# Attention over channels and a GELU layer on one core: an order of issue written out step by step, more seven-product sets, and sums of squares by accumulating DMAs

## The chip, the core and the metric

The kernel runs on one NeuronCore of a Trainium2 chip. PE (TensorE) multiplies matrices, ACT (ScalarE) applies functions, DVE (VectorE) does elementwise arithmetic and transposes of 32 by 32 tiles, POOL (GpSimd) and SP (SyncE) mostly issue DMAs. Each engine works through its own queue in order; semaphores tie the queues together. Matmul results land in PSUM, eight banks of 128 x 512 fp32; everything else on the core lies in SBUF.

The metric is the device time of one launch in microseconds, the median of several runs. The profile is of one further execution, whose own time is given beside its span.

## The reference

```python
# q, k, v: (4, 6080, 256) fp32; tau = 1; w_in: (256, 2048); w_out: (2048, 256)
qn = q / (norm(q, axis=1) + 1e-6)          # norms over the 6080 tokens
kn = k / (norm(k, axis=1) + 1e-6)
s = kn.transpose(0, 2, 1) @ qn / tau       # (4, 256, 256)
a = exp(s - s.max(-1)); a /= a.sum(-1) + 1e-9
x = (v @ a).reshape(24320, 256)
h = x @ w_in
g = 0.5 * h * (1 + tanh(c * (h + 0.044715 * h**3)))
out = g @ w_out                            # (24320, 256) fp32
```

## The kernel before

**Tiling.** Per batch the attention matrix is only 256 x 256, so the kernel folds it into the first weights: AW = a @ w_in (256 x 2048, bf16), made once a batch. Then h = v @ AW, the GELU, and the product with w_out run over blocks of 512 tokens, 12 to a batch, the last one with 448; 48 blocks in all, numbered n, with block n % 12 of batch n // 12. The 2048 columns of a block are eight *pairs* of two 128-column groups. For one pair `mm1` does four matmuls of 512 columns into a double bank and `gelu` turns it into bf16 in `g`.

**Sets.** Two pairs can be made together in seven half-size products (a Strassen-like scheme over two halves of the tokens, two of the inner dimension and two pairs). `SETS` names the pairs that go together: 1 with 2, and 5 with 6. `small` does product m (1 to 7) as two matmuls of 256 columns, into a double bank `qp` or into the single bank `rb` (tag "s"). The steps between are in `set_step`: cq and y5 are copies on ACT, ap and ax are additions on DVE, Gq, Gr and Gx the GELUs of the parts. `sums_w` prepares differences of AW once a batch, `sums_v` differences of v once a block. Blocks 0 and 1 of all have no sets, block 2 has one, blocks 10 and 11 of the first three batches have none, every other block has two (`sets_of`).

**Second product.** The product with w_out is always done in seven products, M1 to M7, each in two halves A and B of four matmuls with 256 columns, into banks "r" and "p". T1 to T4 are the differences of g that it needs (`sums_1`, `sums_2`, on DVE); cq, y5, ap, ax, c11a are copies and additions of its results, c11 to c22 the transposes into the output tile, after the fourth of which `store` issues four DMAs on SP. Most of this runs one block after the h that it uses, some of it two.

**The next batch.** While a batch is multiplied, q and k of the next one arrive in chunks of six rows for each partition (`load_one`, on POOL's queue, which converts fp32 to bf16). In blocks 1 to 8 the Gram matrix of q and k is summed in PSUM bank "a" (`gram_row`, row0 to row5), ACT squares the chunk (qsq, ksq), and `fold` adds the squares up on DVE: an addition in bf16 of half the rows to the other half, then three fp32 additions into the running sum ACC of 128 x 512. After the last chunk `ss_cols` sums ACC over the partitions on PE, and a chain of small steps follows in blocks 9 to 11 (`norms`, `k_factors`, `k_row`, `scores_b`, `scores_c`, `row_sums`, `aw_part`), which ends with the next AW.

**Order.** The scheduler is off: instructions stand on each engine in the order in which the program issues them. Before, three lists of steps served all blocks: `GRAM`, `PLAIN` and `NO_SETS` (L604 to L620). A step like "M1A-1" means M1A of the block before; "w0m1" product 1 of set 0; "g3" and "G3" matmuls and GELU of pair 3; "vs+1" the differences of v of the next block. `todo` keeps a set of what is done, and `extras` hangs loads and the chain on the steps e0 to e7. "w" steps of a set that a block does not have turn into `mm1` and `gelu` of its pairs.

Of the kernel before, what the change touches and what calls it, by code (L numbers as in the profile page):

```python
# [3 lines left out]

# [13 lines left out]
def kernel(  # L18
# [31 lines left out]
    addp = ctx.enter_context(tc.tile_pool(name="addp", bufs=1))  # L50
# [3 lines left out]
    vts = ctx.enter_context(tc.tile_pool(name="vts", bufs=4))  # L54
# [6 lines left out]
    xp = ctx.enter_context(tc.tile_pool(name="xp", bufs=1))  # L61
    cp = ctx.enter_context(tc.tile_pool(name="cp", bufs=1))
# [121 lines left out]
    def fold_rows(b, c):  # L184

        n = len(rows_of(b, c))
        if n == 8:
            a1 = addp.tile([128, 4, 512], BF16, tag="a1")
            nc.vector.tensor_add(a1, SQ[b, c][:, 0:4, :], SQ[b, c][:, 4:8, :])
            SQ[b, c] = a1  # L190
            n = 4
        SQR[b, c] = n
# [3 lines left out]
    def fold(b, c, k):  # L196


        n = len(rows_of(b, c))
        half = n // 2  # L200
        if k == 1:
            sq = SQ.pop((b, c))
            a1 = addp.tile([128, 4, 512], BF16, tag="a1", name=f"a1_{b}_{c}")
            nc.vector.tensor_add(a1[:, 0:half, :], sq[:, 0:half, :], sq[:, half : 2 * half, :])
            terms = [a1[:, i, :] for i in range(half)]
            if n % 2:
                terms.append(sq[:, n - 1, :])
            if b in ACC:
                terms.append(ACC[b])
            FOLD[b, c] = terms  # L210
            return
        terms = FOLD[b, c]
        if len(terms) < 2:
            return
        last = len(terms) == 2
        if last and b not in ACC:
            ACC[b] = accp.tile([128, 512], FP32, tag="acc", name=f"acc{b}")
        o = ACC[b] if last else addp.tile([128, 512], FP32, tag=f"a{2 + k % 2}", name=f"f{k}_{b}_{c}")
        nc.vector.tensor_add(o, terms[0], terms[1])
        FOLD[b, c] = [o] + terms[2:]  # L220
# [37 lines left out]
    def ss_cols(b):  # L258

        SS[b] = pM.tile([128, 4], FP32, tag="a", name=f"ss{b}")  # L260
        for j in range(4):
            nc.tensor.matmul(SS[b][:, j : j + 1], lhsT=ACC[b][:, j * 128 : j * 128 + 128],
                             rhs=ones_f[:, 0:1], start=True, stop=True)
# [38 lines left out]

    def pe_vt(n, tag):

        ps = pM.tile([128, 2, BLK], BF16, tag=tag, name=f"vt_ps{n}")
# [4 lines left out]
        vT = vts.tile([128, 2, BLK], BF16, tag="vT", name=f"vT_pe{n}")  # L310
        nc.vector.tensor_copy(vT[:, 0, :], ps[:, 0, :])
        nc.vector.tensor_copy(vT[:, 1, :], ps[:, 1, :])
        vt_tiles[n] = vT
# [35 lines left out]
    def norms(b):  # L349

        sv = smx.tile([128, 4], FP32, tag="sv")
        nc.vector.tensor_copy(sv, SS[b])
        rt = smx.tile([128, 4], FP32, tag="rt")
        nc.gpsimd.tensor_tensor(rt, sv, halves, op=ALU.pow)
# [20 lines left out]
    def k_row_pe(b):  # L375
        dg, rh = NRM[b]
        ps = pM.tile([128, 256], FP32, tag="a", name=f"rk{b}")
        nc.tensor.matmul(ps, lhsT=ones_f, rhs=dg, start=True, stop=True)
        S = G[b]
        for jc in range(2):  # L380
            nc.vector.tensor_mul(S[:, jc, :], S[:, jc, :], ps)
        NRM[b] = (S, rh)

    def scores_b(b):
        S, rh = NRM.pop(b)
        th = smx.tile([128, 2, 256], FP32, tag="th")
        for jc in range(2):
            nc.scalar.activation(th[:, jc, :], S[:, jc, :], AF.Tanh, scale=rh[:, jc : jc + 1])
        TH[b] = th

    def scores_c(b, step):
# [7 lines left out]
        step -= 1  # L399
        dn = DN[b]  # L400
        piece = dn[:, step // 2, step % 2 * 128 : step % 2 * 128 + 128]
        nc.vector.reciprocal(piece, piece)
        if step == 3:
            eT = smx.tile([128, 2, 256], BF16, tag="eT")
            nc.vector.scalar_tensor_tensor(eT, th, 1.0, dn, op0=ALU.add, op1=ALU.mult)
            ET[b] = eT

    DN = {}

    def row_sums(b):  # L410
        ps = pM.tile([128, 2], FP32, tag="a", name=f"sums{b}")
        for ic in range(2):
            for jc in range(2):
                nc.tensor.matmul(ps[:, ic : ic + 1],
                                 lhsT=ET[b][:, jc, ic * 128 : ic * 128 + 128],
                                 rhs=ones_bf[:, 0:1], start=jc == 0, stop=jc == 1)
        rs = smx.tile([128, 2], FP32, tag="rs")
        nc.vector.reciprocal(rs, ps)
        RS[b] = rs

    AW = {}

    def aw_part(b, fs, ic, eng, tag="a"):
        if b not in AW:
            AW[b] = awp.tile([128, 2, D], BF16, tag="aw", name=f"aw{b}")
        ps = pM.tile([128, 512], FP32, tag=tag)
        for jc in range(2):
            nc.tensor.matmul(ps, lhsT=ET[b][:, jc, ic * 128 : ic * 128 + 128],  # L428
                             rhs=win_bf[:, jc, fs * 512 : fs * 512 + 512],
                             start=jc == 0, stop=jc == 1)  # L430
        o = AW[b][:, ic, fs * 512 : fs * 512 + 512]
        if eng == "act":
# [15 lines left out]
    GS, HP = {}, {}  # L448

# [8 lines left out]
    SIDE = {}  # L458

    def pair_of_banks(n, p, name):  # L460

        if (n, p) not in SIDE:
            side = SIDE.get("next", 0)
            k = sets_of(n)
            if k == len(SETS):
                turns = [x for x in range(PAIRS) if x not in [b for _, b in SETS]]
            else:
                turns = [int(x[1]) if x[0] == "g" else SETS[int(x[1])][x[2:] == "m7"]
                         for x, _ in order_of(n)
                         if x[0] == "g" or x[0] == "w" and (x[2:] == "m5" if int(x[1]) < k else x[2:] in ("m1", "m7"))]  # L470
            for x in turns:
                SIDE[n, x] = side
# [593 lines left out]
```

## Time and profile before

| what | value |
|---|---|
| device time, median of 3 runs | 718.33 us (718.33 to 719.25) |
| profiled execution: its own time, its span | 717.09 us, 715.3 us |
| granted TensorE clock | 0.998 |
| matmuls of `mm1` (L495), of sets (L564), of the second product (L716) | 904, 1106 and 3 narrow ones, 2688 |
| DMA traffic of POOL's queue, of SP's | 39.46 MB, 37.67 MB |
| first matmul, last matmul | at 10.2 us, at 708.3 us |

A row of the groups reads: line, engine, operation, output <- inputs, shape, count | busy us, mean ns of one | idle us of the engine just before, and what ended it. A row of the timeline: start, duration, engine, line, operation, tiles, shape, count of instructions merged into it, and in brackets the idle time before it. A row of DMA issues: output <- input, issuing queue, count, KB each, and the median us from issue to landing.

### The profile page before, as it was taken

What the parts mean: (1) busy time and instruction counts of PE and PEld (TensorE: products, weight loads), DVE (VectorE), ACT (ScalarE), POOL (GpSimd) and SP (SyncE); (2) the same over time, 40 slices, a digit from 0 to 9 for tenths busy, and PEclk for the clock granted to TensorE, in tenths of its full rate; (3) what the DMA queues carried; (4) which work ended last, traced back from release to release, by engine and by line L of the source; (5) the groups of instructions that cost most, each with busy time, mean ns of one, the idle gap of its engine ahead of it and who ended that gap; (6) DMA issues with size and microseconds to landing.
All of it is one profiled execution on the core that took longest, in us unless ns stands there. A gap on an engine that the chain in (4) does not pass through costs nothing.

```text
span 715.3 us, 13755 instructions
## 1 busy us (share of the span) xinstructions
PE 682.2 (95%) x5335; PEld 515.5 (72%) x5335; DVE 610.5 (85%) x1174; ACT 595.3 (83%) x828; POOL 69.8 (10%) x131
## 2 busy tenths in 40 slices
PE   3898999999999999999999999999999999999995
PEld 2755777777667777777767787777766777777784
DVE  4489799998987999999878899999897788888885
ACT  5387799998768999999868999999876888888883
POOL 4320011100001111010000111110000000000000
PEclk9999999999999999999999999999999999999999
DMA  9999578973567888974557699887355245363414
GB/s 242 207 249 145 97 113 124 131 115 58 98 93 127 106 126 138 135 132 66 93 90 111 104 133 132 125 127 120 58 92 96 49 82 93 64 113 59 72 31 85
DMA packets 162273, 79.28 MB, mean 111 GB/s; under 512 B 150464, under 2 KB 153280, under 8 KB 161216
## 3 DMA queue, kind: packets, MB, share of 16 engines
q0 software_dynamic: 13440, 39.46, 34.5%
q1 hardware_dynamic: 147664, 37.67, 32.5%
q10 hardware_dynamic: 1104, 1.28, 0.5%
q8 instruction: 41, 0.67, 0.4%
q14 instruction: 24, 0.20, 0.1%
HBM read 78.91 MB, written 36.83 MB: 162 GB/s over the span
## 4 chain that ended last, share of the span: by engine, by line
PE 79%; DVE 11%; DMA 6%; issue 2%; ACT 1%; POOL 0%; DVEq 0%; POOLq 0%; ACTq 0%
PE h L495 22%; PE r L716 20%; PE p L716 15%; PE rb L564 9%; PE qp L564 7%; PE G L230 4%; DMA t<-in_k_dram 3%; DMA wst<-in_moe_w_out_dram 2%; PE ps L428 2%; DVE ot L740 1%; DMA t<-in_q_dram 1%; DVE t L677 1%; DVE t L693 1%; DVE t L689 1%; DVE t L691 1%
## 5 line engine op out<-in xcount | busy, mean ns | idle before, releaser
L716 PEld LDWEIGHTS <-wcomb 128*128 128x128 bf16 x2688 | 262.1, 98 | 63.0 <-issue 8.1
L505 ACT ACTIVATE g<-h 128x1024 bf16<-128x1024 f32 (+1 forms) x226 | 227.6, 1011 | 43.6 <-PE h L495 41.0
L495 PE MATMUL h<-vT,aw 128*128 128x512 bf16 (+1 forms) x840 | 212.1, 375 | 0.7 <-ACT g L584 0.7
L716 PE MATMUL r<-t,wcomb 128*128 128x256 bf16 (+1 forms) x1152 | 164.7, 271 | 3.1 <-DVE c L731 2.5
L495 PEld LDWEIGHTS <-aw 128*128 128x128 bf16 x904 | 88.4, 98 | 65.6 <-issue 1.6
L716 PE MATMUL p<-g,wcomb 128*128 128x256 bf16 (+1 forms) x704 | 94.2, 271 | 0.0
L584 ACT ACTIVATE g<-qp 128x1024 bf16<-128x1024 f32 (+1 forms) x79 | 80.2, 1015 | 9.5 <-PE qp L564 9.2
L176 ACT ACTIVATE sq<-t 128x1536 bf16<-128x1536 bf16 (+4 forms) x59 | 79.5, 1361 | 9.6 <-DMA t<-in_q_dram 9.6
L564 PEld LDWEIGHTS <-sw 128*128 128x128 bf16 x632 | 61.5, 98 | 29.0 <-issue 5.3
L579 DVE TENSOR_TENSOR qp<-rb,yw 128x512 f32<-128x512 f32 (+1 forms) x79 | 54.9, 695 | 24.9 <-ACT x L725 16.1
L691 DVE TENSOR_TENSOR t<-g 128x1024 bf16<-128x1024 bf16 (+1 forms) x96 | 64.5, 672 | 0.0
L693 DVE TENSOR_TENSOR t<-t,g 128x1024 bf16<-128x1024 bf16 (+1 forms) x96 | 64.3, 670 | 0.0
L564 PE MATMUL rb<-tv,sw 128*128 128x256 bf16 (+1 forms) x316 | 60.1, 272 | 3.6 <-DVE qp L579 3.4
L230 PE MATMUL G<-t 128*128 128x256 bf16 (+1 forms) x368 | 60.5, 272 | 2.0 <-DMA t<-in_k_dram 1.9
L582 DVE TENSOR_TENSOR xw<-rb,yw 128x512 f32<-128x512 f32 (+1 forms) x79 | 54.3, 687 | 8.7 <-PE rb L564 8.1
L689 DVE TENSOR_TENSOR t<-g,t 128x1024 bf16<-128x1024 bf16 (+1 forms) x96 | 60.9, 666 | 0.0
L589 ACT ACTIVATE g<-rb 128x512 bf16<-128x512 f32 (+1 forms) x79 | 47.1, 597 | 16.4 <-PE rb L564 13.9
L136 POOL DMA_DIRECT2D vb<-in_v_dram x46 | 23.1, 502 | 356.6 <-PE h L495 356.6
L677 DVE TENSOR_TENSOR t<-g 128x2048 bf16<-128x2048 bf16 (+1 forms) x48 | 57.1, 1190 | 0.2 <-ACT g L592 0.2
L716 PE MATMUL r<-g,wcomb 128*128 128x256 bf16 (+1 forms) x384 | 55.9, 271 | 0.3 <-DVE ot L740 0.3
L716 PE MATMUL p<-t,wcomb 128*128 128x256 bf16 (+1 forms) x384 | 52.1, 271 | 1.5 <-DVE c L731 1.5
L574 ACT ACTIVATE qp<-rb 128x512 f32<-128x512 f32 (+1 forms) x79 | 46.4, 588 | 5.5 <-PE rb L564 2.4
(127 smaller groups left out, 852.2 us busy)
## 6 DMA issues: line engine op xcount, KB each, us to landing
out_dram<-ot SPq DMA_DIRECT2D x176, 128.0 KB, 3.2
vb<-in_v_dram POOLq DMA_DIRECT2D x42, 256.0 KB, 5.2
t<-in_q_dram POOLq DMA_DIRECT2D x22, 384.0 KB, 7.0
t<-in_k_dram POOLq DMA_DIRECT2D x22, 384.0 KB, 4.6
wst<-in_moe_w_out_dram POOLq DMA_DIRECT2D x2, 1024.0 KB, 10.9
t<-in_q_dram POOLq DMA_DIRECT2D x3, 512.0 KB, 14.9
t<-in_k_dram POOLq DMA_DIRECT2D x3, 512.0 KB, 16.7
out_dram<-ot SPq DMA_DIRECT2D x12, 112.0 KB, 2.5
```

Source lines behind the costliest of these rows:

```text
L176: nc.scalar.activation(o, t[:np_, r, :], AF.Square)
L230: nc.tensor.matmul(G[b][:, jc, :], lhsT=qt[:np_, r, jc * 128 : jc * 128 + 128], rhs=kt[:np_, r, :], start=first and jc == 0, stop=jc == 1, ...
L495: mm = nc.tensor.matmul(hp[:, u, :cols], lhsT=AW[b][:, cc, fc * 128 : fc * 128 + 128], rhs=vt_tiles[n][:, cc, :cols], start=cc == 0, stop= ...
L505: nc.scalar.activation(gs(n)[:, 2 * p : 2 * p + 2, :cols], HP.pop((n, p))[:, :, :cols], AF.Gelu_apprx_tanh)
L564: nc.tensor.matmul(acc[:, u * hc : u * hc + hc], lhsT=lhs[:, u * 128 : u * 128 + 128], rhs=rhs, start=m in (1, 5) and u == 0, stop=u == 1, ...
L579: nc.vector.tensor_add(qp(n, i)[:, 1, :c], RB[n, i][:, :c], YW[n, i][:, :c])
L584: nc.scalar.activation(gs(n)[:, 2 * pa : 2 * pa + 2, :c].rearrange("p u (t x) -> p t u x", t=2), QP.pop((n, i))[:, :, :c].rearrange("p t ( ...
L677: nc.vector.tensor_sub(t1[:, :, :hc], quarter(n, 0, 1), quarter(n, 0, 0))
L689: nc.vector.tensor_sub(o, quarter(n, 1, 1, f0, f1), ts[1][:, f0:f1, :hc])
L691: nc.vector.tensor_sub(o, quarter(n, 1, 1, f0, f1), quarter(n, 0, 1, f0, f1))
L693: nc.vector.tensor_sub(o, ts[2][:, f0:f1, :hc], quarter(n, 1, 0, f0, f1))
L716: nc.tensor.matmul(ACCS[n, acc][:, :hc], lhsT=wcomb[:, w, fc, :], rhs=x, start=first and k == 0, stop=k == 3, skip_group_check=True)
```

## The change

All lists and the machinery around them go. A string of steps stands for each block: 31 strings, and `WINDOW` says which of them block n uses (those of blocks 8 to 19 serve the second and third batch too). A step is now one instruction or a tight group on one engine, and the loop does nothing but run them in order. Three of the strings stand below.

Blocks 10 and 11 get two sets as the others have; blocks of the last batch get three, with pairs 4 and 7 in the third, whose weight differences lie in the buffers of the squares. The banks of sets' `rb` are "s" and "s", and "s", "a", "s" in the last batch. The tiles of ap and ax (`yw`, `xw`) lie in buffers of q and k in the last batch, and `yw` gets two buffers elsewhere.

`fold` keeps its bf16 addition, of three rows to three. Its result goes by a DMA from POOL's queue into ACC, now 128 x 3 x 512 fp32: a plain converting copy for the first chunk, an accumulating one for the seven others. `fold_last` (fl1, fl2) adds the three parts on DVE before `ss_cols`. The transposed tiles of v have three buffers instead of four. The last block's end keeps another order of its products.

```diff
-    vts = ctx.enter_context(tc.tile_pool(name="vts", bufs=4))
+    vts = ctx.enter_context(tc.tile_pool(name="vts", bufs=3))
...
-    def fold(b, c, k):
...
-        o = ACC[b] if last else addp.tile([128, 512], FP32, tag=f"a{2 + k % 2}", name=f"f{k}_{b}_{c}")
-        nc.vector.tensor_add(o, terms[0], terms[1])
-        FOLD[b, c] = [o] + terms[2:]
+    def fold(b, c):
+        assert len(rows_of(b, c)) == 6
+        sq = SQ.pop((b, c))
+        a1 = a1p.tile([128, 3, 512], BF16, tag="a1", name=f"a1_{b}_{c}")
+        nc.vector.tensor_add(a1, sq[:, 0:3, :], sq[:, 3:6, :])
+        FOLD[b, c] = a1
+
+    def fold_dma(b, c):
+        first = b not in ACC
+        if first:
+            ACC[b] = accp.tile([128, 3, 512], FP32, tag="acc", name=f"acc{b}")
+        nc.gpsimd.dma_start(out=ACC[b], in_=FOLD.pop((b, c)),
+                            **({} if first else {"accum_op": ALU.add}))
+
+    def fold_last(b, i):
+        nc.vector.tensor_add(ACC[b][:, 0], ACC[b][:, 0], ACC[b][:, i])
...
+    SIDE = ({0: 0, 2: 0, 4: 0, 6: 0}, {0: 0, 3: 0, 5: 0, 7: 0}, {0: 0, 3: 0, 5: 0}, {0: 0, 5: 0, 3: 0})
+    R_BANK = ("", "s", "ss", "sas")
...
     def sets_of(n):
-        blk = n % NB
-        if n == 2:
-            return 1
-        if n < 2:
-            return 0
-        return 0 if n // NB < B - 1 and blk in (10, 11) else 2
+        return (0, 0, 1)[n] if n < 3 else 3 if n // NB == B - 1 else 2
...
-    SETS = ((1, 2), (5, 6))
+    SETS = ((1, 2), (5, 6), (4, 7))
...
+    def set_buffer(n, i, xy):
+        if n // NB == B - 1:
+            return qkp.tile([128, 512], FP32, tag="qk"[xy == "x"], name=f"{xy}w{n}_{i}")
+        return {"x": xp, "y": ywp}[xy].tile([128, 512], FP32, tag=f"{xy}w", name=f"{xy}w{n}_{i}")
...
+        def loads(n, p):
             b, blk = divmod(n, NB)
             gate = GATE[0]
             if p == 0 and PE_BLOCKS <= n + 2 < NN:
                 load_vt(n + 2)
             if p == 0 and n + 3 < NN:
                 cast_v(n + 3, gate)
+            if p in (2, 5) and b + 1 < B and blk < len(chunks_of(b + 1)):
+                load_one(b + 1, blk, p // 5, gate)
...
         for n in range(NN):
+            for x in ORDER[WINDOW[n]].split():
+                m = re.match(r"([A-Za-z]+\d*[A-Za-z]*\d?)(?:([+-])(\d+))?$", x)
+                step(m[1], n + {None: 0, "+": 1, "-": -1}[m[2]] * int(m[3] or 0))
+
+WINDOW = [
+    0, 1, 2, 3, 4, 5, 6, 7, 8, 9, 10, 11, 12, 13, 14, 15, 16, 17, 18, 19, 8, 9, 10, 11,
+    12, 13, 14, 15, 16, 17, 18, 19, 8, 9, 20, 21, 22, 23, 24, 25, 26, 27, 27, 27, 27, 28,
+    29, 30,
+]
+ORDER = [
...
+    """g0 w0cq c11a-2 w0y5 e0 row2-1 w0m6 G0 row4 w0ap row4-1 row1-1 M1B-1 T2b-1 ksq e2 w0m7
+    M1A-1 T3a-1 g3 w0ax cq-1 M5B-1 T3b-1 G3 w0m4 M5A-1 c11-2 T4b-1 w0m3 w0Gr w0m2 row1 e5
+    T4a-1 w0Gq w1m5 M6A-1 c22-2 w1m1 vs+1 M6B-1 y5-1 w1cq g4 ap-1 w1y5 w1m6 qsq row5-1 w1ap
+    M3A-1 M3B-1 w1m3 c12-1 w1m7 w0Gx row5 f1 w1m2 G4 M7A-1 M2B-1 w1ax fd M2A-1 w1Gq T1a M7B-1
+    w1m4 w1Gx g7 ax-1 w1Gr c22-1""",
+    """g0 G7-1 c11a-2 T3a-1 e0 w0m1 row3-1 G0 T2a-1 M4B-2 row0-1 T2b-1 w0m5 M4A-2 w0cq e2 row2-1
+    c21-2 M5A-1 w0y5 fl1 w0m6 g3 w0ap M5B-1 fl2 G3 w0m7 M1A-1 w0ax w0m2 gc M1B-1 vs+1 y5-1 e5
+    w0m4 w0m3 w0Gr ss T4b-1 cq-1 c11-2 w0Gq w1m5 sv w1m1 T3b-1 M6B-1 pow M6A-1 T4a-1 w1cq g4
+    w1y5 ap-1 kf w0Gx w1m6 M3A-1 G4 w1ap M7B-1 T1a M7A-1 kr w1m7 g7 ax-1 w1ax krp G7 w1m2 S0+1
+    M3B-1 S1+1 w1m3 w1Gx w1m4 c12-1 w0m5+1 w1Gr vs+2 M4A-1 M4B-1 w1Gq T3b M2B-1 c21-1 w0m1+1
+    M2A-1 T3a w0cq+1""",
...
+    """g0 T1a-1 w2Gr-1 e0 w1m1 G0 M4A-2 c11a-2 w0m5 w0m1 T3a-1 M4B-2 w0cq e2 M5B-1 c21-2 w0y5
+    w1m5 T2a-1 w0m6 w2Gx-1 M5A-1 w0ap M1A-1 w1y5 M1B-1 T2b-1 w1cq w0m7 cq-1 w0m2 w0ax w0m3
+    y5-1 w1m6 e5 w0Gq M6A-1 w1ap w0m4 M6B-1 T3b-1 w0Gr w1m7 w2m5 ap-1 w1m2 w2y5 w1m3 w1ax w2m1
+    M3A-1 w2cq vs+1 M3B-1 w1Gq M7B-1 c12-1 w2m6 c11-2 M7A-1 w1Gx w2ap w1m4 w0Gx g3 c22-2 w1Gr
+    T4b-1 w2m7 G3 w2m3 w2ax M2A-1 w2m2 ax-1 M2B-1 w2Gq T4a-1 w2m4""",
...
+]
```

The strings shown are those of block 8 and block 9 of a batch, where the last chunk is added and the chain of the next batch begins, and the one of four blocks of the last batch.

## The prediction

> **What bounds the kernel now.** I read the busy table first, then busy time by stage, then the rows of the operations that the change counts up or down, then the DMA issues.
>
> ```profile
> PE 682.2 (95%) x5335; PEld 515.5 (72%) x5335; DVE 610.5 (85%) x1174; ACT 595.3 (83%) x828; POOL 69.8 (10%) x131
> ```
>
> PE is busy 95% of the span, but these are averages. The view of busy time by stretch (us; PE, PEld, DVE, ACT, POOL with counts, then clock, DMA share, GB/s) shows where the other 5% is:
>
> ```profile
> 40.00:80.00 40.00, 35.73 (x238) 22.69 (x236) 33.27 (x60) 30.39 (x36) 4.70 (x9) 1.00 0.91 171
> 80.00:160.00 80.00, 80.00 (x646) 62.86 (x645) 75.12 (x144) 75.78 (x104) 9.54 (x18) 1.00 0.81 121
> 160.00:200.00 40.00, 37.90 (x276) 26.73 (x274) 35.25 (x67) 30.65 (x47) 2.57 (x4) 1.00 0.48 83
> ...
> 560.00:700.00 140.00, 140.00 (x1120) 109.10 (x1118) 119.19 (x230) 119.73 (x179) 3.89 (x8) 1.00 0.40 68
> ```
>
> In the long stretches (the blocks with Gram rows at 80 to 160, the last batch at 560 to 700) PE is never free. It is free in the start and around the joint of two batches (160 to 200). In the Gram stretch VectorE and ScalarE stand at 94 and 95%; in the last batch both have 15% left. Is "never free" also "at its peak"? Matmul records overlap, so I take starts in the timeline of PE:
>
> ```profile
> 632.74 1.04 PE L716 MATMUL p<-g,wcomb 128*128 128x256 bf16 x8
> 633.61 0.38 PE L564 MATMUL rb<-vT,aw 128*128 128x256 bf16 x2
> 633.83 0.60 PE L716 MATMUL r<-t,wcomb 128*128 128x256 bf16 x4
> 634.27 1.03 PE L495 MATMUL h<-vT,aw 128*128 128x512 bf16 x4
> 635.13 0.38 PE L564 MATMUL rb<-tv,sw 128*128 128x256 bf16 x2
> ```
>
> Eight matmuls of 256 columns take 633.61 - 632.74 = 0.87 us, 0.109 each; four of 512 take 0.86, 0.216 each. Time goes by columns, with almost nothing per instruction. **A rule of the Trainium skill speaks against using this:** "Perfetto Trace Analysis", section "Identifying the Most-Contended Engine", says that matmul busy share misleads and that the weight-load share tells the headroom. That is 62.86/80 = 79% in the Gram stretch and 78% in the last batch: by the rule a fifth of PE is free, other engines bind, and columns taken away give 0. By the start times PE has nothing left there, and columns count in full. I go by the start times.
>
> Start to start, PE's idle time comes to 11.4 us around the three joints (4.3 in 160 to 260, 3.8 in 320 to 400, 3.3 in 500 to 560), 5.2 in 40 to 80, and 1.4 after 700.
>
> **The change, part by part.**
>
> *More sets.* A set makes two pairs of 128-column groups with 14 matmuls of 256 columns in place of 8 of 512: 14 x 0.1087 = 1.52 against 8 x 0.216 = 1.73 us of PE, 0.206 less. By the two instruction lists there are 24 more: two in each of blocks 10 and 11 of three batches (12), a third in each block of the last batch (12); 7 of them have 448 columns. PE: 17 x 0.206 + 7 x 0.18 = **-4.8 us**, all of it where PE is busy or waits little. What the others pay:
>
> ```profile
> L505 ACT ACTIVATE g<-h 128x1024 bf16<-128x1024 f32 x198 | 202.3, 1024 | 32.2 <-PE h L495 30.2 <-DVE aw L435 1.8
> L584 ACT ACTIVATE g<-qp 128x1024 bf16<-128x1024 f32 x77 | 78.3, 1017 | 8.7 <-PE qp L564 8.4
> L579 DVE TENSOR_TENSOR qp<-rb,yw 128x512 f32<-128x512 f32 x77 | 53.7, 697 | 24.1 <-ACT x L725 16.1 <-ACT yw L577 8.0
> L582 DVE TENSOR_TENSOR xw<-rb,yw 128x512 f32<-128x512 f32 x77 | 53.0, 689 | 8.2 <-PE rb L564 7.7
> ```
>
> ScalarE: two GELUs (2.05) become copy 0.59, copy 0.60, GELUs 1.02, 0.60 and 0.62 (rows L574, L577, L584, L589, L592): +1.37 a set. VectorE: +0.70 + 0.69 = 1.39. A block of the last batch lasts 12.65 us (the casts of v start at 627.95 and 640.59). ScalarE and VectorE are busy there 119.73/140 and 119.19/140 of it, 10.8 each. A third set makes that 12.2 at most, PE's columns 12.65 - 0.21 = 12.4. It fits, by 0.2 us. The third set has its own bank for its neighbour ("a", free when no Gram runs), so its chain of PE, ScalarE, VectorE and PE again does not queue behind the first two. If the cover fails by 0.25 us a block, 12 x 0.25 = 3 us eat the gain.
>
> *Sums of squares.* The row L219 goes, 69 fp32 additions (24 + 21 + 21 + 3), about 47.1 us of VectorE:
>
> ```profile
> L219 DVE TENSOR_TENSOR f<-a x24: 684/686/693, 67.5 to 505.4; 128x512 f32<-128x512 bf16 x24
> L219 DVE TENSOR_TENSOR f<-f,a x21: 650/678/681, 88.1 to 506.7; 128x512 f32<-128x512 f32 x21
> L219 DVE TENSOR_TENSOR acc<-f,acc x21: 684/685/693, 94.3 to 507.4; 128x512 f32<-128x512 f32 x21
> ```
>
> Six return at the ends (4.1). With 33.3 for the sets, 5.9 for six more blocks' differences of v and 1.2 for one more weight set, VectorE does 47.1 - 44.5 = 2.6 us less in all, but 2 us less in each Gram block and more at the joints and in the last batch. ScalarE does +33.0 - 2.7 (copies of the old order without sets) + 1.5 (one square moved to it) = 31.8 more, 88% of the span. Worth to PE of VectorE's relief in the Gram blocks: 0, PE never waited there.
>
> Added are 24 DMAs on POOL's queue, some 0.54 us of issue each as its other DMAs (13 us more, POOL is at 10%). POOL holds each until VectorE's addition and the former accumulation are done; behind it stand loads of q, k and casts of v. Neighbours are 8 us or more apart but for chunks 4 and 5 (7 us), and what waits has a block of slack: 0. **The dangerous wait** is VectorE's first closing addition of each batch, which needs the last accumulation landed. Behind it stands the addition that the next set's matmul needs. Counting PE's columns in the list from the last issue to that addition gives 5.2 us. How long does an accumulation take? No row shows one. It writes 128 x 1536 fp32, 786 KB, and reads as much again. Near rows (last column: us from issue to landing):
>
> ```profile
> vb<-in_v_dram POOLq DMA_DIRECT2D x42, 256.0 KB, 5.2
> t<-in_q_dram POOLq DMA_DIRECT2D x22, 384.0 KB, 7.0
> t<-in_k_dram POOLq DMA_DIRECT2D x22, 384.0 KB, 4.6
> wst<-in_moe_w_out_dram POOLq DMA_DIRECT2D x2, 1024.0 KB, 10.9
> t<-in_q_dram POOLq DMA_DIRECT2D x3, 512.0 KB, 14.9
> ```
>
> The skill's "DMA: Bandwidth & Descriptors", section "Anatomy of one DMA", fits 2.0 us + bytes/436 GB/s: 3.8 us, an estimate from that page, no wait. By the rows of q and k, which read 786 KB too, it is 4.6 to 7.0; the largest row allows 14.9, in the crowded start. I take 7.0: no q or k is loaded in that block, but the destination is read as well. With 0.5 for the issue VectorE waits 2.3. PE has up to 1.5 us of other work in the list (m6, g3, M5B) before the matmul that needs VectorE's next addition; I take 1.3 as its lead, so PE loses 1.0: **+3 us** for three batches (bounds 0 and, at 14.9, +27).
>
> *One list for all blocks.* Steps now stand singly: the softmax chain of the next batch is cut into single instructions over blocks 9 to 11, factors and copies apart from their matmuls. The waits that it can remove are those 11.4 us, such as 0.49 at 168.0 behind four folds of L219, 0.62 at 170.7, 0.75 at 196.7 where PE has just made row sums and stands before the reciprocal. From rows' spacings every block of the new list needs more PE than VectorE or ScalarE time, but four by 0.5 at most and block 11 of the first batch (VectorE 13.7, PE 11.8, it prepares two weight sets): +1. I take 60% of the joints' idle as gone, **-7**; bounds 0 and -11.4. In the start weights' preparation and the first sets are cut apart too: half of 5.2, **-2.5**. Against it I set 0.05 us a block for unevenness, +1.8: the old orders left 0.00. At the end the last product is now followed by an addition and a transpose, before by a transpose alone: +0.4. Pools: v's transposed tiles go from 4 buffers to 3; the load for block n+2 then waits for block n-1's last matmul, and has 18 us to land in 5.5: 0.
>
> Sum: -4.8 + 3 - 7 + 1 - 2.5 + 1.8 + 0.4 = -8.1. The profiled execution took 717.09 (span 715.3 and 1.8 around it), so 709.0; the median of the runs shown, 718.33, is 1.2 above it: **710**.
>
> **Rivals.**
> 1. *Only the columns pay.* New waits at the joints replace the old: 718.3 - 4.8 + small losses = 714. For it: VectorE is the fuller engine at the joints (35.25 of 40), and sets add work just there. Against: four folds leave that very place.
> 2. *The accumulation is late* (the slower side). Each batch loses the landing less 6.0 us (5.2 + 1.3 - 0.5). The rest of the change brings 11.1, so it decides from a loss of 3.7 a batch, a landing near 9.7 us. At 12 to 15: 3 x 6 to 3 x 9 = 18 to 27, some 725 to 734. For it: 10.9 and 14.9 in the rows. Against: DMA share is 0.48 there, 1.06 in the start.
> 3. *ScalarE binds.* With 88% on average and 95% in Gram blocks the one-by-one order leaves 0.2 to 0.3 us of PE idle in 36 blocks, 7 to 11 us: 717 to 722.
> 4. *The change does less than it says:* by the lists it has 103 sets against 79 and 24 accumulations, so this is out.
>
> **How the numbers follow.** Forecast 0.54; rival 1 0.15; rival 2 0.16; rival 3 0.15 (half of it slower, a third the same). A difference under 0.2% (1.4 us) can't be told from none. Faster: 0.54 + 0.15 + 0.02 = 0.71; same 0.06; slower 0.23. The forecast's own range is 703 (all joints gone) to 715. To hold 8 in 10 it goes from 702 to 722, which leaves out most of rival 2.
>
> **What would show it.** Right: PE's records of the h matmuls fall from 904 to 712, PE idle near 160 to 200 halves, blocks of the last batch start 12.4 us apart. The dangerous wait is the idle time before the addition into acc, released by a DMA: under 3 us each. I am wrong if that is above 5, if ScalarE is at 97% or more in Gram blocks with PE idle beside it, or if blocks of the last batch stay at 12.65.

## The result, and the profile after

| what | before | after |
|---|---|---|
| device time, median (lowest to highest), four runs each | 718.33 us (717.46 to 719.25) | 713.95 us (712.45 to 715.93) |
| profiled execution: its own time, its span | 717.09, 715.3 us | 714.2, 712.3 us |
| granted TensorE clock | 0.998 | 0.990 |

The ratio is 0.994, with an interval from 0.9913 to 0.9968: the changed kernel is 4.4 us faster, about half of what was forecast. A run over 1.5% above the fastest of its kernel counts as slow and is left out of ratios, though not of medians: one of e1 (714.05 us), one of e12 (807.62) and one of before (1207.34, beside e5 to e8). The first lines of the page after, busy time and the clock in 40 slices of 17.8 us:

```profile
PE 680.7 (96%) x5479; PEld 532.1 (75%) x5479; DVE 608.6 (85%) x1180; ACT 618.5 (87%) x894; POOL 92.0 (13%) x155
...
PEclk9998999999999999999999999999999999999999
```

VectorE has 1.9 us less, as worked out (2.6). ScalarE's rows add up to 31.1 more, as worked out (31.8); its busy time, in which overlapping records count once, rose by 23.2. POOL has 22 more, not 13. PE's busy time hardly fell, though its work shrank by the columns of 24 sets. The row of the clock, which the prediction never used, says why one should look further: it has an 8 in its fourth slice, and the mean clock went down. Busy time by stretch of the kernel after (us; PE, PEld, DVE, ACT, POOL with counts, then clock, DMA share, GB/s):

```profile
40.00:60.00 20.00, 13.31 (x62) 6.30 (x61) 12.87 (x21) 8.92 (x9) 1.62 (x3) 0.84 0.80 194
...
100.00:120.00 20.00, 16.51 (x121) 12.26 (x120) 11.51 (x22) 14.35 (x19) 3.01 (x5) 0.91 0.85 176
80.00:160.00 80.00, 76.51 (x600) 59.14 (x598) 64.24 (x121) 72.11 (x94) 14.12 (x23) 0.98 0.96 173
160.00:200.00 40.00, 39.84 (x316) 30.77 (x314) 36.95 (x74) 35.64 (x57) 4.82 (x6) 1.00 0.66 125
560.00:700.00 140.00, 140.00 (x1203) 117.33 (x1202) 134.21 (x259) 132.34 (x214) 3.90 (x8) 1.00 0.46 77
```

The joint at 160 to 200, where 2.1 us of 40 were idle, is full. The last batch was full and is full: its blocks start 12.42 us apart where they started 12.64 apart. Two places are new. At 40 to 60 PE is busy 13.31 of 20 us at a clock of 0.84, and at 100 to 120 it is busy 16.51 at 0.91. The same two stretches of before:

```profile
40.00:60.00 20.00, 18.03 (x112) 10.34 (x110) 17.63 (x26) 17.33 (x20) 3.12 (x6) 1.00 1.11 220
100.00:120.00 20.00, 20.00 (x166) 16.01 (x165) 19.26 (x38) 19.05 (x27) 2.11 (x4) 1.00 0.95 137
```

PE's waits in the kernel after (us in all, how often, the longest) name what held it there (the row of 10.5 is the start of the kernel, and before has it too):

```profile
PE G L225 <- ACT first L122: 10.5, 1, 10.5
PE rb L570 <- DMA vT<-vb: 6.7, 1, 6.7
PE G L225 <- DMA t<-in_k_dram: 4.1, 2, 3.5
```

PE's timeline around the first of them (start, duration, operation, count, idle time before it):

```profile
47.11 1.03 PE L494 MATMUL h<-vT_pe,aw 128*128 128x512 bf16 x4
54.83 0.59 PE L570 MATMUL rb<-vT,aw 128*128 128x256 bf16 x2 [6.69 <-DMA vT<-vb]
55.21 1.91 PE L494 MATMUL h<-vT_pe,aw 128*128 128x512 bf16 x4
56.92 1.91 PE L700 MATMUL r<-g,wcomb 128*128 128x256 bf16 x8
58.63 2.76 PE L494 MATMUL h<-vT_pe,aw 128*128 128x512 bf16 x8
61.22 1.04 PE L700 MATMUL p<-t,wcomb 128*128 128x256 bf16 x8
```

The `rb` at 54.83 is product 1 of block 2. The string of block 0 has it as "w0m1+2", two blocks ahead of its own, and the transposed v of block 2 had not landed. Its transpose was issued on SP at 48.7 us, when PE had waited for half a microsecond, and landed 6.0 us later. In before the same tile is first read at 62.5 us, by VectorE, and product 1 comes at 66.3. The wait also costs after it has ended: eight matmuls of 256 columns take 58.63 - 56.92 = 1.71 us, 0.214 each, where the prediction's timeline showed 0.109. PE runs at half its rate until about 60.3 us, and loses 2.7 us more.

At the second place the timeline is of the same form:

```profile
100.13 1.04 PE L700 MATMUL r<-t,wcomb 128*128 128x256 bf16 x8
104.66 0.53 PE L225 MATMUL G<-t 128*128 128x256 bf16 x2 [3.49 <-DMA t<-in_k_dram]
104.98 0.63 PE L570 MATMUL rb<-tv,sw 128*128 128x256 bf16 x2
105.41 1.91 PE L494 MATMUL h<-vT,aw 128*128 128x512 bf16 x4
```

A Gram row waits for a chunk of k, and four matmuls of 512 columns then take 1.71 us (107.12, the next start, less 105.41). That chunk was issued at 92.55 us and took 12.1 us to land. Most of what was issued beside it was late too: two transposes of v took 11.9 and 13.6 us, a chunk of q 11.7, the first copy into ACC 11.1, four stores 12.2 in the median. In before a chunk of k issued at 91.3 us landed in 4.5; the next four stores came 5 us after it, here 1 us before.

Measured from start to start of matmuls, PE's idle time (half rate counted in) was 25.6 us and is 26.6: 9.6 in place of 5.2 at the start, 5.3 new at 100 to 108, 1.9 in place of 11.4 around the joints, 0.8 in place of 1.4 after 700, the rest before 40 us and in pieces under 0.3. With 4.8 us of columns gone that makes -3.8; the first matmul comes 0.25 us later and the end after the last one is 0.36 longer, so -3.2, beside -3.0 between the spans.

The sums of squares: the tile ACC after, with what the closing additions waited for and the landing of the accumulations (lowest, median, highest us), and below it three rows of DMA issues from the page:

```profile
L211 POOL DMA_DIRECT2D acc<-a x24: 530/890/927, 91.4 to 504.8; - x24
...
L215 DVE TENSOR_TENSOR acc<-acc x6: 680/687/694, 178.1 to 511.6; 128x512 f32<-128x512 f32 x6
...
DVE acc L215: 0.2, 1
...
DMA to landing us min/median/max: 5.0/6.5/11.1
```

```profile
acc<-a POOLq DMA_DIRECT2D x24, 768.0 KB, 6.5
...
t<-in_q_dram POOLq DMA_DIRECT2D x22, 384.0 KB, 6.3
t<-in_k_dram POOLq DMA_DIRECT2D x22, 384.0 KB, 6.1
```

The dangerous wait is 0.2 us in the whole kernel. But k's median landing rose from 4.6 to 6.1 us; e6 and e12 below ask what raised it.

### The profile page after: what moved, and what is told of

Read it like the earlier page. It is cut to its first block, busy times and chain, and to the rows that moved or that the text cites. A ratio compares the mean times of both kernels' runs of the same rounds, so it can differ in the third digit from the quotient of the medians.

```text
span 712.3 us, 14365 instructions
## 1 busy us (share of the span) xinstructions
PE 680.7 (96%) x5479; PEld 532.1 (75%) x5479; DVE 608.6 (85%) x1180; ACT 618.5 (87%) x894; POOL 92.0 (13%) x155
## 4 chain that ended last, share of the span: by engine, by line
PE 52%; issue 1%; DMA 1%; DVE 1%; POOL 0%; ACT 0%; DVEq 0%; POOLq 0%
PE r L700 14%; PE p L700 10%; PE h L494 10%; PE rb L570 8%; PE qp L570 6%; PE G L225 2%; DMA t<-in_k_dram 1%; PE awp L434 1%; PE ss L257 0%; DMA acc<-a 0%; PE rk L379 0%; POOL vb L138 0%; DVE c L716 0%; DVE qp L591 0%; DVE t L675 0%
## 5 line engine op out<-in xcount | busy, mean ns | idle before, releaser
L504 ACT ACTIVATE g<-h 128x1024 bf16<-128x1024 f32 (+1 forms) x178 | 179.3, 1014 | 33.6 <-PE h L494 31.3
L494 PE MATMUL h<-vT,aw 128*128 128x512 bf16 (+1 forms) x648 | 165.0, 378 | 0.0
L596 ACT ACTIVATE g<-qp 128x1024 bf16<-128x1024 f32 (+1 forms) x103 | 104.5, 1016 | 6.4 <-PE qp L570 5.0
L494 PEld LDWEIGHTS <-aw 128*128 128x128 bf16 x712 | 70.3, 99 | 50.5 <-issue 2.2
L570 PEld LDWEIGHTS <-sw 128*128 128x128 bf16 x824 | 80.6, 98 | 21.1 <-issue 0.6
L591 DVE TENSOR_TENSOR qp<-rb,yw 128x512 f32<-128x512 f32 (+1 forms) x103 | 71.1, 690 | 20.5 <-PE rb L570 10.0
L594 DVE TENSOR_TENSOR xw<-rb,yw 128x512 f32<-128x512 f32 (+1 forms) x103 | 69.7, 677 | 16.0 <-PE rb L570 14.1
L570 PE MATMUL rb<-tv,sw 128*128 128x256 bf16 (+1 forms) x412 | 78.2, 272 | 0.0
L570 PEld LDWEIGHTS <-aw 128*128 128x128 bf16 x618 | 60.1, 98 | 23.1 <-issue 8.4
L586 ACT ACTIVATE qp<-rb 128x512 f32<-128x512 f32 (+1 forms) x103 | 60.3, 585 | 10.6 <-PE rb L570 5.4
L589 ACT ACTIVATE yw<-qp 128x512 f32<-128x512 f32 (+1 forms) x103 | 61.1, 593 | 4.6 <-PE qp L570 2.1
L604 ACT ACTIVATE g<-xw 128x512 bf16<-128x512 f32 (+1 forms) x103 | 63.1, 624 | 0.2 <-DVE xw L594 0.2
```

The source lines that it names most:

```text
L494: mm = nc.tensor.matmul(hp[:, u, :cols], lhsT=AW[b][:, cc, fc * 128 : fc * 128 + 128], rhs=vt_tiles[n][:, cc, :cols], start=cc == 0, stop= ...
L504: nc.scalar.activation(gs(n)[:, 2 * p : 2 * p + 2, :cols], HP.pop((n, p))[:, :, :cols], AF.Gelu_apprx_tanh)
L570: GATE[0] = nc.tensor.matmul(acc[:, u * hc : u * hc + hc], lhsT=lhs[:, u * 128 : u * 128 + 128], rhs=rhs, start=m in (1, 5) and u == 0, st ...
L591: nc.vector.tensor_add(qp(n, i)[:, 1, :c], RB[n, i][:, :c], YW[n, i][:, :c])
L594: nc.vector.tensor_add(XW[n, i][:, :c], RB[n, i][:, :c], YW.pop((n, i))[:, :c])
L596: nc.scalar.activation(gs(n)[:, 2 * pa : 2 * pa + 2, :c].rearrange("p u (t x) -> p t u x", t=2), QP.pop((n, i))[:, :, :c].rearrange("p t ( ...
```

## The experiments

My theory after the result: the mechanisms forecast for the joints and the last batch hold in full, and two waits for transfers early in the kernel, with the half rate behind them, took the other half of the gain. Against it stand: that the slow rate has a cause of its own; that the k transfer was late because of an instruction ahead of it on POOL's queue; and that the gain came from less VectorE work or from the lists, and not from the columns. The times of before in the groups of runs that follow had medians of 717.2 to 717.8 us, about 1 us less than beside the changed kernel (718.33), so a microsecond between groups decides nothing.

### Product 1 of block 2 issued a block later (e1_m1_later)

The step leaves the last lines of block 0's string for those of block 1's.

```diff
-    T1a G5 vtp G4 g7 vtc1 vtc0 e5 w0m1+2 pA11 G7 g6 pF0 M1A G6 M1B pS1 g1+1 pA12 pF1""",
+    T1a G5 vtp G4 g7 vtc1 vtc0 e5 pA11 G7 g6 pF0 M1A G6 M1B pS1 g1+1 pA12 pF1""",
...
-    T1a w0m5+1 row0 w0cq+1 M3B-1""",
+    T1a w0m1+1 w0m5+1 row0 w0cq+1 M3B-1""",
```

> One step moved: product 1 of block 2's first set goes from the end of block 0's list to just before its product 5 at the end of block 1's list. Theory A (the loss in the changed kernel is two single waits of PE for transfers that a step asks for too early; the one at 47.8 us costs 6.9 us of waiting and 2.7 us of matmuls at half rate after it): that wait goes, some 2 us of the start's other waits come back, 706 to 708 us. Theory B (the start is bound by the transfers and the preparation of the weights, and the early step only shows it): the wait turns up at the first products of block 1 or 2, 712 to 714 us.

Measured: 705.11 us (701.14 to 714.05), ratio 0.981 (0.977 to 0.985). The stretch of its start:

```profile
40.00:60.00 20.00, 19.89 (x118) 11.15 (x119) 18.78 (x31) 16.74 (x19) 3.21 (x6) 1.00 1.08 244
```

PE is full at full clock where it had 13.31 us at 0.84. One step in the wrong place cost about 9 us, the 9.4 of wait and half rate. In its profile the waits for k fell to 2.5 us, the longest 1.5 (at the place of the 3.5), with no half rate after that. The chunk of k that had taken 12.1 us took 10.1.

### Gram rows of block 4 behind other work (e2_rows_later), and both edits (e4_both)

In block 4 row3, row5 and row4, which need the late chunk, move behind row0 and row2 of the list's middle.

```diff
-    """g0 fd-2 T2b-1 w0y5 e0 w0m6 G0 M4A-2 w0ap M4B-2 row3 qsq-1 c21-2 w0m7 g3 e2 w0ax T2a-1 w0m3
-    G3 M1B-1 c11a-2 row5 w0m2 T4a-1 row0-1 qsq row4-1 w0m4 T3b-1 M1A-1 vs+1 M5B-1 w0Gr row4 e5
-    w1m5 T4b-1 w0Gq row0 row2-1 w1m1 M5A-1 cq-1 row5-1 w1cq g4 w1y5 w1m6 w0Gx M6A-1 w1ap G4
+    """g0 fd-2 T2b-1 w0y5 e0 w0m6 G0 M4A-2 w0ap M4B-2 qsq-1 c21-2 w0m7 g3 e2 w0ax T2a-1 w0m3
+    G3 M1B-1 c11a-2 w0m2 T4a-1 row0-1 qsq row4-1 w0m4 T3b-1 M1A-1 vs+1 M5B-1 w0Gr e5
+    w1m5 T4b-1 w0Gq row0 row2-1 row4 row3 row5 w1m1 M5A-1 cq-1 row5-1 w1cq g4 w1y5 w1m6 w0Gx M6A-1 w1ap G4
```

> The Gram rows 3, 4 and 5 of block 4's list moved some 4 to 5 us of PE's columns later, nothing else. Theory A: the wait at 100.9 us (3.7 us) and the half rate after it (1.7) go: 708 to 709.5 us. Theory B (the accumulating DMAs keep the engines so full that whatever needs q and k next waits): the wait moves to the rows of the next block or to the transposed v, 712 us or more.

> The moves of the two kernels with the step of product 1 and with the Gram rows together. Theory A: the gains add, 714 - 8 - 5.3 = 700 to 703 us, TensorE's granted clock back at 0.998, PE never idle for over 1 us after 45 us. Theory B: 707 us or more.

Measured: alone 711.12 us (709.70 to 717.33), between the two expectations. Its profile, of its slowest execution, still waits 7.9 us for k, now in six places of at most 2.2 us, the longest with half rate behind it (163.8 to 167.4 us): the long wait went, others came, and k's chunk took 14.3 us. With both edits 700.85 us (699.94 to 701.84), ratio 0.977 (0.975 to 0.979), 13 us under the changed kernel and 2.3% under the one before: **the best version of the study**. Its waits for k and two stretches:

```profile
PE G L225 <- DMA t<-in_k_dram: 2.9, 3, 1.3
```

```profile
40.00:60.00 20.00, 19.89 (x116) 10.91 (x116) 18.21 (x31) 16.16 (x19) 3.21 (x6) 1.00 1.07 239
...
80.00:160.00 80.00, 79.26 (x630) 62.36 (x640) 68.61 (x129) 76.54 (x105) 15.39 (x24) 1.00 1.05 197
```

The clock is 1.00 in both; at 80 to 160 the DMA engines are busy all the time (share 1.05), and PE loses under 1 us by busy time. The runs that follow start from this version where they say so.

### The copy ahead of k on POOL's queue (e3_copy_after_k)

The timeline of POOL has the first chunk's copy into ACC at 91.44, just ahead of k at 92.55. Here it goes behind k.

```diff
-    T4b-1 cq-1 c22-2 w0m2 f1-2 G3 M5A-1 M6A-1 c11-2 M5B-1 fd-2 w0Gq vs+1 w1m1 w1m5 e5 M6B-1
+    T4b-1 cq-1 c22-2 w0m2 f1-2 G3 M5A-1 M6A-1 c11-2 M5B-1 w0Gq vs+1 w1m1 w1m5 e5 fd-2 M6B-1
```

> The first DMA of sums of the first batch (a plain converting copy) goes behind the load of k on POOL's queue, in block 3's list. If the copy ahead of k is what made k land 12.1 us after its issue: k lands in 7 us or less, the wait at 100.9 goes, 708 to 709.5 us. If it is the crowd of everything that moves then (transposes of v, eight stores, q, a cast): k still takes 10 us or more and the time stays within 1 us of 714.

Measured: 714.32 us (711.64 to 720.91), no better than the changed kernel. The chunk of k still took 10.1 us and the waits for k came to 6.0 us in five places. Order on the queue is not what makes k late. The first wait is not it either: with product 1 a block later this chunk took 9.6 to 13.9 us in seven versions, with the early step 10.1 to 14.3 in five. What all twelve share, and before does not, is that four stores are issued about 1 us ahead of this k; in five of their traces these took 9 to 12 us themselves. That they make k late fits, but no run moved them alone. The wait is then a matter of slack: the Gram row stands 8.6 us behind k's issue in the changed kernel and in e1, so a landing of 12.1 us costs 3.5 and one of 10.1 costs 1.5.

### Busy during the wait (e5_busy_wait)

On the changed kernel, 60 matmuls of zeros, 256 columns each, fill most of the 6.7 us. They write the bank that product 1 of block 2 then overwrites.

```diff
+            if (n, i) == (2, 0):
+                for _ in range(60):
+                    nc.tensor.matmul(RB[n, i][:, 0:256], lhsT=ones_bf, rhs=zeros_bf, start=True, stop=True)
```

> The changed kernel with 60 matmuls of zeros (256 columns, 6.5 us) put in front of the early product of block 2, into the bank that this product then overwrites: PE waits for the same transfer, but at work. If idle PE is what halves the matmul rate after the wait, the stretch from 54.8 to 60 us runs at 0.109 us a matmul, the granted clock is back near 0.995 and the time is 2 to 3 us lower, 711 to 712. If the slow stretch has another cause (the crowded transfers, the place in the program), it stays and the time is 714 or above.

Measured: 711.66 us (709.99 to 715.84). With 60 matmuls more the median is 2.3 us lower, but the ranges of the two kernels overlap, and so do their intervals against before (0.9899 to 0.9945 here, 0.9913 to 0.9968 there). What does not overlap is the granted clock of the runs: 0.992 to 0.997 in these eight, 0.988 to 0.990 in the four of the changed kernel. PE's timeline, of its slowest execution:

```profile
48.19 6.72 PE L560 MATMUL rb<-zeros_bf,ones_bf 128*128 128x256 bf16 x60
57.15 0.38 PE L573 MATMUL rb<-vT,aw 128*128 128x256 bf16 x2 [2.23 <-DMA vT<-vb]
57.36 1.54 PE L494 MATMUL h<-vT_pe,aw 128*128 128x512 bf16 x4
58.69 1.92 PE L703 MATMUL r<-g,wcomb 128*128 128x256 bf16 x8
60.40 2.27 PE L494 MATMUL h<-vT_pe,aw 128*128 128x512 bf16 x8
```

In this execution the transfer landed at 57.2, 2.3 us later than in the profile of the changed kernel, so 2.2 us stayed idle, and some 3 us at half rate followed (58.69 to 60.40 for eight of 256 columns, 1.71 us again). The clock of the runs speaks for idleness as the cause of the slow rate; this trace does not show the clean case, without any idle time. The Trainium skill, "TensorE: Matmul & The Clock Gate", section "What's actually happening", says that the clock falls to a half after an idle window of about 3.4 us and comes back after as long a busy one, in windows that run free. Slow stretches of 3.4 and 5.5 us after 3.5 and 6.7 us idle fit roughly. That 2.2 us idle was enough does not: by that page's length this wait would have been free of it. Nor does length alone decide, for waits of 2.6 us (e3, at 116.7), 2.7 (e8, at 150.6) and 3.0 (e6, at 102.9) had full rate behind them.

### The sums of squares back on VectorE (e6_dve_after, e7_dve_moved, e10_dve_split), or by DMA in the old order (e12_before_dma)

e6 is the changed kernel and e7 is e4_both, with this edit; e10 is e7 with each addition cut in three of 512 elements, spread over VectorE's next steps.

```diff
-        nc.gpsimd.dma_start(out=ACC[b], in_=FOLD.pop((b, c)),
-                            **({} if first else {"accum_op": ALU.add}))
+        a1 = FOLD.pop((b, c))
+        if first:
+            nc.vector.tensor_copy(ACC[b], a1)
+        else:
+            nc.vector.tensor_add(ACC[b], ACC[b], a1)
```

> The changed kernel with its 24 DMAs of sums replaced by one VectorE addition each (1536 fp32, the first of a batch a copy), at the same places of the list; the order is otherwise the changed one. If the accumulating DMAs make q and k late: k of block 3 lands in 8 us or less, PE's waits for q and k fall from 4.1 us to under 1, 708 to 710 us, with the wait at 47.8 left as it is. If the crowd is there without them: PE still waits 3 us or more near 100 us, and VectorE's 1.7 us more per Gram block come on top, 714 to 717.

> The kernel with both moves (700.85) and VectorE additions instead of the DMAs of sums. If VectorE's relief in the Gram blocks is worth nothing to PE, as predicted, and the DMAs only cost waits: 698 to 701. If the relief is what lets the joints run full (VectorE 85 to 96% there): PE idle comes back at the joints and the time is 704 or more.

> The kernel with VectorE additions instead of the DMAs of sums and both moves (718.0), the addition of 1536 cut into three of 512, spread over the next VectorE steps of the list. If it was the length of one instruction (1.75 us in front of additions that PE waits for) that cost 17 us: most comes back, 703 to 707. If it is VectorE's load as such: 714 or more.

Measured: e6 727.87 us (727.55 to 733.16), 14 above the changed kernel; e7 718.02 (717.63 to 718.42), 17.2 above e4_both; e10 719.14 (718.87 to 719.60). No expectation had such a size. e6 also answers what it was made for. Without any accumulating DMA, PE still waits 3.0 us for the chunk of k at 102.9 us, which took 11.8; its waits for k, and k's landing:

```profile
PE G L228 <- DMA t<-in_k_dram: 4.7, 4, 3.0
...
t<-in_k_dram POOLq DMA_DIRECT2D x22, 384.0 KB, 6.0
```

So the wait for k at 100 to 108 us, and the rise of the median from 4.6 to 6.1, came with the new order and not with the accumulations. Now to the 17 us. The addition, PE's waits and a stretch of Gram blocks of e7, then the same stretch of e4_both and of before:

```profile
L215 DVE TENSOR_TENSOR acc<-acc,a x21: 1717/1750/1754, 89.9 to 508.0; 128x1536 f32<-128x1536 f32 x21
```

```profile
PE rb L573 <- DVE qp L594: 8.7, 12, 1.4
PE p L703 <- DVE p L753: 4.6, 5, 1.2
```

```profile
260.00:340.00 80.00, 75.78 (x596) 57.85 (x595) 74.49 (x127) 72.60 (x99) 8.39 (x16) 1.00 0.68 111
```

```profile
260.00:340.00 80.00, 79.38 (x630) 62.50 (x639) 71.01 (x138) 75.42 (x107) 14.76 (x22) 1.00 0.92 180
```

```profile
260.00:340.00 80.00, 79.51 (x634) 61.68 (x633) 76.45 (x145) 76.06 (x106) 8.91 (x17) 1.00 0.78 116
```

VectorE goes from 71.01 to 74.49 of 80 us, and PE waits for it 13 us in the kernel, nearly all in the Gram blocks (0.5 us at each joint). e10 excludes the length of one instruction as the reason: cut in three, the additions cost the same. In before VectorE was fuller still in this stretch (76.45 of 80), and PE hardly waited. The likely reading is that these strings were made for less VectorE work in the blocks that have the sums; no run fitted a new order to the additions. The runs of e7 and of e10 lie within 0.8 us of each other, those of e4_both within 1.9, of the changed kernel within 3.5, of e6 within 5.6, and those of e1, e8 and e11 within 9 to 13; what makes this scatter was not found.

The opposite part alone, in before with its own lists: the fp32 additions become the DMAs, issued with the bf16 addition, and two closing additions stand ahead of the sums over partitions.

```diff
     def fold(b, c, k):
...
+        if k != 1:
+            return
...
+        nc.vector.tensor_add(a1, sq[:, 0:3, :], sq[:, 3:6, :])
...
+        nc.gpsimd.dma_start(out=ACC[b], in_=a1, **({} if first else {"accum_op": ALU.add}))
...
-            (9, 3): [ss_cols, norms],
+            (9, 3): [fold_last, ss_cols, norms],
```

> The kernel before with its own three lists and sets, only the fp32 additions of the sums replaced by the accumulating DMA behind the bf16 addition, and two closing additions before the sums over partitions. If VectorE's relief is worth nothing where PE never waited, as predicted: 716.5 to 718.5. If the folds at the joints made PE's waits there: 3 x 1.1 us less, 714 to 715. If the transfers crowd as in the changed kernel: 719 or more, with PE waiting for q and k.

Measured: 724.44 us (723.88 to 807.62; the three others up to 724.61) against 717.4, ratio 1.009 (1.007 to 1.011). PE's waits in it, then k's landing, then two waits of before:

```profile
PE G L220 <- DMA t<-in_k_dram: 5.2, 8, 1.8
PE ss L252 <- DVE acc L210: 3.0, 3, 1.0
...
t<-in_k_dram POOLq DMA_DIRECT2D x22, 384.0 KB, 4.6
```

```profile
PE rb L564 <- DVE qp L579: 3.4, 4, 1.5
...
PE G L230 <- DMA t<-in_k_dram: 1.9, 2, 1.4
```

VectorE's relief does bring something: the 3.4 us that PE waited for `qp` in before, at the start and the joints, are gone, with 0.9 for ScalarE's part of `qp` in their place. It is outweighed. Waits for k come to 5.2 us instead of 1.9, though k's median landing stays at 4.6, and stores land in 4.1 instead of 3.2 us. The closing additions cost 3.0, and after two of these three waits (at 344.0 and 517.9 us, 1.0 each) PE's matmuls ran at half rate for some 3.3 us, which loses 1.7 each. Together -2.5 + 3.3 + 3.0 + 3.4 = 7.2, the difference of the spans. Across the versions the parts do not add up:

| | old lists and sets | new strings, more sets (start mended) |
|---|---|---|
| sums on VectorE | 717.2 to 717.8 (before) | 718.0 (e7) |
| sums by DMA | 724.4 (e12) | 700.85 (e4) |

Each part alone gives nothing or loses 7 us; together they give 17. e12's additions are cut otherwise than e7's, so the table shows the size of what only the whole gives, not its exact amount.

### Sets taken away (e8_two_sets, e9_no_sets_joint)

On e4_both. e8 leaves the third set out of the blocks of the last batch, e9 all sets out of blocks 10 and 11 of the first three; the pairs are made by `mm1` and `gelu` at the places of products 1 and 7 and of two steps of the set. In e9 pair 6 of these blocks takes bank "h".

```diff
+        NOSET = lambda n, i: n // NB == B - 1 and i == 2
...
+            elif what[0] == "w" and NOSET(n, int(what[1])):
+                pair = SETS[int(what[1])]
+                if what[2:] in ("m1", "m7"):
+                    mm1(n, pair[what[2:] == "m7"])
+                elif what[2:] in ("cq", "Gq"):
+                    gelu(n, pair[what[2:] == "Gq"])
```

> The kernel with both moves (700.85), the last batch with two sets instead of three: pairs 4 and 7 by four matmuls of 512 columns and a GELU each, at the places of the third set's products 1 and 7 and its GELUs. If PE's columns count in full: 12 x 0.206 = 2.4 us more, 703.0 to 703.5. If weight loads tell PE's headroom (84% in the last batch with three sets): no more than 700.9, since ScalarE and VectorE are relieved.

> The kernel with both moves (700.85), blocks 10 and 11 of the first three batches again without sets: their pairs 1, 2, 5 and 6 by four matmuls of 512 columns and a GELU each, at the places of the sets' products 1 and 7. If the sets there pay by their columns alone: 12 sets less, 2.4 us more, 703 to 704. If VectorE, at 96% in these stretches, is what the sets cost and the step-by-step order alone would do: 700 or less. If the list there only fits with sets: 706 or more.

Measured: e8 706.78 us (702.89 to 712.57), e9 707.75 (705.29 to 713.89). Both scatter, from waits for k in the profiled run of e8 (6.3 us), so the stages are read instead of the totals. Blocks of e8's last batch start 12.85 us apart, those of e4_both 12.42: 0.21 by columns, and 0.22 of small waits (before's own lists make two sets in 12.64). The same stretch of e8, and then of e4_both:

```profile
560.00:690.00 130.00, 129.45 (x1018) 99.28 (x1017) 109.88 (x214) 108.94 (x164) 3.42 (x7) 1.00 0.43 73
```

```profile
560.00:690.00 130.00, 129.25 (x1105) 108.58 (x1112) 124.78 (x243) 120.35 (x196) 3.42 (x7) 1.00 0.42 72
```

The third set adds 9.3 us of weight loads, 14.9 of VectorE and 11.4 of ScalarE to these 130 us, and the blocks are shorter. In e9 twelve blocks of a middle batch last 167.48 us where e4_both needs 165.78: 0.82 by columns, the rest new waits, as for ScalarE:

```profile
PE h L494 <- ACT g L504: 1.6, 6, 0.3
```

### One more Gram row moved (e11_row_of_8)

On e4_both, row4 of block 8 goes from the front of its string to row1 in the middle, since e4_both waited there.

```diff
-    """g0 w0cq c11a-2 w0y5 e0 row2-1 w0m6 G0 row4 w0ap row4-1 row1-1 M1B-1 T2b-1 ksq e2 w0m7
-    M1A-1 T3a-1 g3 w0ax cq-1 M5B-1 T3b-1 G3 w0m4 M5A-1 c11-2 T4b-1 w0m3 w0Gr w0m2 row1 e5
+    """g0 w0cq c11a-2 w0y5 e0 row2-1 w0m6 G0 w0ap row4-1 row1-1 M1B-1 T2b-1 ksq e2 w0m7
+    M1A-1 T3a-1 g3 w0ax cq-1 M5B-1 T3b-1 G3 w0m4 M5A-1 c11-2 T4b-1 w0m3 w0Gr w0m2 row1 row4 e5
```

> The kernel with both moves (700.85), and in the list of block 8 row 4 of the last chunk some 2.5 us of PE's columns later, beside row 1. If the waits of 0.3 to 2.8 us for k at the start of block 8 of each batch are what is left to gain: 698 to 700 us and PE's waits for k under 1 us in all. If transfers slip further whatever is moved: 700.5 or more.

Measured: 701.86 us (700.05 to 709.42), no gain. Its waits at block 8 are gone, and its profile has 2.6 us of waits for k elsewhere, 1.5 of them at 95 us, nearly as much as e4_both's 2.9. Whether such waits make the 9 us between e11's runs was not measured, since only one of them has a trace.

## Why the forecast had the sign and half the size

**Columns, -4.8: right.** The period of the last batch fell by 0.22 us, as the start times said (0.21; the casts named there lie 12.64 apart, not 12.65). The rule on weight loads was against it: their share rose from 78% to 117.33/140 = 84% while the blocks grew shorter, and e8 shows the same with the third set alone. Here it does not give PE's headroom.

**Joints, -7: too small.** Their idle time went from 11.4 to 1.9 us, -9.5. Without sets in blocks 10 and 11 (e9) 0.9 us a joint comes back beyond the columns, so the sets are a part of it; which of the chain's steps filled the rest was not taken apart.

**Late accumulation, +3: did not come.** The landing was taken at 7.0 us from the rows of q and k, and the median of the 24 is 6.5; the last of each batch, which decide, took 5.3 to 5.6, with no q or k loaded then. The closing additions waited 0.2 us in all. The largest row, 14.9, belonged to another stage, as the text said; the page's estimate of 3.8 was below every one of the 24.

**The start, -2.5: the first failed step.** It became +4.4. "Half of 5.2" was taken from the kind of edit, without a look at what the moved steps need. The string of block 0 has "w0m1+2". The only sentence on the landing of v, "has 18 us to land in 5.5: 0", holds for blocks in steady state; block 2 in a start with a DMA share of 1.1 is not such a block. e1 shows that this one step is worth 9 us.

**"What waits has a block of slack: 0": the second failed step.** The first Gram row of the late chunk stands 8.6 us behind k's issue, not a block, and k took 12.1: 3.5 us of wait and 1.7 of half rate, 5.3 as measured from start to start. The sentence was written of what stands behind the accumulations, but they are not what made this chunk late: without them it took 11.8 (e6) and 9.6 us (e7), in before 4.5. The new order brings k close behind four stores, and that was given no cost at all. The 24 transfers of 768 KB did raise the DMA share at 80 to 160 us from 0.81 to 0.96. What they add to the waits for k is 3.3 us in the old lists (e12) and 1.7 in the mended new ones (2.9 in e4_both, 1.2 in e7).

**VectorE's relief "worth 0": true of the Gram blocks of the old lists, false of the new.** In e12 the waits for VectorE that went, 3.4 us, were at the start and the joints. With the new strings the relief is worth 17 us (e7). The sum used a price of the old order in the new one. The total was not hurt, since both came together, but a reader who had dropped the DMAs on the strength of that sentence would have lost all.

**Block 11, unevenness and end, +3.2 together: about 1.4.** The end took 0.4, 0.6 of idle after 700 us went, and the pieces before 40 us and under 0.3 came to 1.4, with a first matmul 0.25 later. ScalarE did not bind (rival 3): where it stands highest, 76.80 of 80 us in the Gram blocks of a middle batch, PE waits for transfers if for anything.

Put together with what was measured: -4.8 - 9.5 + 4.4 + 5.3 + 1.4 = -3.2, where the sum had -8.1. The time is that of rival 1 (714) in size and not in mechanism: the joints paid in full. They gave 2.5 us more than the sum had, the accumulation 3 and the small terms 1.8; against these 7.3 stand the 6.9 and 5.3 of the two failed steps. The signs named for a right forecast all came (712 matmuls of h, the joint, 12.42 us), but that the total fell into the range is in part luck: misses of 7 us one way and 12 the other nearly cancelled.

## What to carry to other kernels

When a step is moved ahead, write down when its data is issued and lands in that very place, by the rows of that stage and with what travels beside it: one step two blocks early in a crowded start undid more than all sets brought. A wait of PE can cost more than its own length (here up to 2.7 us more, at half rate after it), so the clock by stretch is read before any story about engines. An order written step by step is fitted to the loads that it was written for; taking one part of such a change alone, in either direction, shows little of its worth in the whole.

## What the runs showed of the hardware

- After PE idled for 6.7 and 3.5 us (the kernel after) and 2.2 us (e5), its matmuls ran at half rate (0.214 us instead of 0.109 for 256 columns) for about 5.5, 3.4 and 3 us. After 2.6 (e3), 2.7 (e8) and 3.0 us (e6) they did not, nor after waits of 1.9 us and less, except two of the three of 1.0 us in e12, each followed by eight matmuls of one column (0.9 us).
- An accumulating DMA of 128 x 1536 from bf16 in SBUF into fp32 in SBUF landed in 5.3 to 10.4 us, median 6.5 (21 of them); the three plain converting copies took 5.0, 5.8 and 11.1. On POOL the issue of one lasts 0.89 us and that of a plain copy 0.53, where the prediction had 0.54 for all; the next issue behind it can start after 0.57 (at 103.08 and 103.65 us).
- The same chunk of k, 384 KB, landed in 9.6 (e7) to 14.3 us (e2) in all twelve versions with the new strings, with or without accumulating DMAs, and a chunk issued at the same time in before in 4.5 us.
